# Block-sparse attention and a low-rank mixer MLP on one core: mixer sums on 32-column groups, more turns by the crossbar, a new order

## The chip, the cores and the metric

One core of a Trainium2 chip runs the whole program in one launch. The metric is the device time in microseconds (us); lower is better. A core has five engines with queues of their own: TensorE (PE in the profile, its weight loads PEld), VectorE (DVE), ScalarE (ACT), GpSimd (POOL) and SyncE (SP), which here only issues DMAs. SP and ACT can issue the DMA that turns a tile through the crossbar (DMA_TRANSPOSE).

## The reference

```python
# B, H, S, D = 4, 8, 768, 64; blocks of 32 positions
scores = q @ k.T / 8
mask   = neighbouring blocks, first and last block row and column, and 3 drawn blocks per block row
attn   = softmax(where(mask, scores, -1e9)) @ v
x = attn with the heads side by side                 # [B, 768, 512]
h = x.transpose(0, 2, 1) @ U @ V                     # U [768, 32], V [32, 768]
u = x + h.transpose(0, 2, 1)
out = u + relu(u @ w_ch1) @ w_ch2                    # 512 -> 2048 -> 512
```

Inputs and output are float32; the kernel computes in float16 with float32 sums.

## The kernel before, in words

Heads are taken in pairs: four pairs per batch, 16 in all, so pair `i` is batch `i // 4`. A sequence is held as 128 partitions by 6 chunks (`T = 6`).

The order of TensorE, VectorE, ScalarE and SP is written out by hand: the text `PLAN` is read word by word. An upper-case letter issues a TensorE step (its digit is the PSUM bank), a lower-case letter the work on another engine that takes up the oldest result of its kind. GpSimd's order is left to the framework's scheduler. The steps:

- `S` (`score`): scores of one chunk of keys of one head of batch 0, two matmuls of 384 columns; `e`: the exp on ScalarE. In batch 0 the mask is inside the contraction, as extra rows (`qres`, `kres`).
- `Q`, `H` (`two_halves`, `quad`): from batch 1 on, scores of two chunks for both heads or one; a head has 64 contraction rows, so the two heads use the two halves of the array's rows. `e` is an exp over 1536 columns, `p` a multiplication by the mask on VectorE.
- `K`, `k`: the parts of that mask.
- `A`, `V` (line 398): probabilities times values, per chunk or per head; `v` (`divide`): reciprocal and two multiplications into `xh` (float16) and `xf` (float32).
- `R` (`turn_qk`, line 644): turns q or k of a pair on TensorE, `t` copies it out. Pairs 1 to 5 are turned so; from pair 6 on `front` does it by two crossbar DMAs on SP. `Z`, `z` do the second head of pair 0.
- `M` (`mix`, line 482): `xh` times U, six matmuls per pair with U padded to 128 columns; `m` copies the result to `a16`.
- `D`, `d` (`add`): V times `a16`, three matmuls per half; two additions on VectorE, into `u16` and `xf`. After the second half `u16` is turned by the crossbar into `uT`, and from pair 4 on `loads` of the next pair is called there. `X`, `Y`, `y`, `E`, `g`: the same on TensorE for pairs 2 and 3. `T`, `x` (`turn`, line 551): pair 15's `u16` turned on TensorE.
- `U` (`w1`, line 569): four matmuls of 384 columns and a relu on ScalarE (`a`) or VectorE (`b`). The first six are in two parts: `P` with three of the four pairs, `C` with the last.
- `W` (`w2`, line 593): four matmuls of 512 columns; four `W` make one output chunk, then `f` adds `xf` and stores. The last chunk is in two halves, `L` and `l` (`last_half`, line 613). Output tiles `of` come from `opool`, which has two buffers.

`loads(i)` issues on SP the q, k and v loads of pair `i + 2` and, from pair 5 on, ahead of them the crossbar turns of pair `i + 1`; GpSimd casts what was loaded. GpSimd also issues the casting loads of W1 (behind the casts of pairs 2 and 3) and of W2 (behind those of pairs 5 and 6). `begin(i)` calls `loads(i)` when the first score of pair 0 to 4 comes up.

Of the kernel before, what the change touches and what calls it, by code (L numbers as in the profile page):

```python
# [2 lines left out]

# [18 lines left out]
def kernel(  # L22
# [43 lines left out]
    small_np = np.concatenate(  # L66
        [(ms_np - 1.0) * -MASK_BIAS, ii[:, None].astype(np.float32)], axis=1
    )

    small_dr = nc.inline_tensor(small_np, name="small_const")  # L70
    eye_dr = nc.inline_tensor(np.eye(P, dtype=np.float16), name="eye_const")
# [37 lines left out]
    small = consts.tile([P, NB + 1], FP32)  # L109
    ms = small[0:NB, 0:NB]  # L110
    iota = small[0:NB, NB:]
    id16 = consts.tile([P, P], FP16)
# [19 lines left out]
    def cast(i, dst, ld):  # L132

        if i < NPE:
            return nc.gpsimd.tensor_copy(out=dst, in_=ld)
        for h in range(2):
            for ts in (slice(0, T // 2), slice(T // 2, T)):
                last = nc.gpsimd.tensor_copy(out=dst[:, h, ts], in_=ld[:, h, ts])  # L138
        return last
# [25 lines left out]
    NPE = HP + 2  # L165
# [64 lines left out]
    with tc.manual_schedule(  # L230
# [14 lines left out]
        nc.scalar.dma_start(out=small[0:NB], in_=small_dr.ap())  # L245
        first_load(0, 1, nc.scalar)
        nc.scalar.dma_start(out=id16, in_=eye_dr.ap())
# [54 lines left out]
        first_cast(0, 0, nc.vector.tensor_copy)  # L302
        first_cast(0, 1, nc.scalar.copy)
        first_turn(1, 0)
        first_row(1, 0, nc.scalar.copy)
        mask_half(0)
        for c in range(2):
            first_turn(0, c)
            first_row(0, c, nc.scalar.copy)
        mask_row(0, 0, nc.vector.tensor_copy)  # L310
        first_turn(1, 1)
# [68 lines left out]
    slots_of = {}  # L380

    def take_est(i, h, j):

        n = free_est.pop(0)
        for u in range(2):
            slots_of[i, h, 2 * j + u] = n + u
        return n

    def drop_est(i, h, g):
        n = slots_of.pop((i, h, g))  # L390
        if g % 2:
            free_est.append(n - 1)
# [14 lines left out]
    class Batch:  # L407
        def __init__(self):
            self.xf = xpool.tile([P, T, HD], FP32, tag="xf", name="xf", bufs=2)
            self.a16 = misc.tile([P, HD], FP16, tag="a16", name="a16", bufs=2)  # L410
            self.uT = [
                upool.tile([P, S], FP16, tag=f"uT{cc}", name=f"uT{cc}")
                for cc in range(NCC)
            ]
# [6 lines left out]
    S0 S3 e Z7 e z S0 S5 e Z2 e A7 z S3 A A e S0 S5 e A R2 e S3 t R1 e A A t S5 v e S3 S1 e K6  # L421
    A0 e A k K5 S3 k A e S6 S1 e K5 A e A k A S3 v K6 R7 e k S1 t e S3 S5 e R0 e S1 t A7 A e S3
    A A e S5 K0 K2 e A k A k S3 v A0 A e S1 A S5 e A K7 e S3 k K1 R2 e k A S5 t R7 e S3 t A S1 e
    v M6 e K5 S3 m k A7 A e S1 A A e S3 D0 A e S5 d R2 e S3 t A S0 e v M6 e D2 m S3 d A5 A e S0
    K7 A e S3 k A K6 e S0 k A A e S3 v R2 e S6 t S0 e S3 e A5 A e A D7 A K6 d S1 k D0 A e S3 d
    M7 e S1 m X6 A e S3 v Y A7 e S0 y E2 A e S3 g X5 Y e E6 A y A g A A Q v R6 e e t M7 X6 m Y p
    H y R7 e p H t U6 e p H b U7 e p H b P6 p e E2 V7 g p C Q v a V6 e e U7 v p P0 a M1 C P2 m p
    a C U6 a D7 Q a d D6 e e d U7 b U6 p U0 b U7 p a E6 Q a g U7 e e U6 b P7 b p X2 C V0 a p V4
    v P5 v Y P7 y C C M0 a a W6 m D7 Q d W e e D7 W d p W U7 f p Q a U7 e e W6 b U7 p U0 b W p a
    Q W e e W p U2 f V7 a p Q v V6 e e U7 v p U0 a U2 b U6 p a M7 a Q m D7 e e W6 d W p D7 W d p  # L430
    Q W e e W7 f p U0 V6 b p V1 v U2 v U0 a U4 a M5 a U6 m D0 U1 a d D6 W a d Q U6 e e W b W p
    W6 f p Q W e e U7 W p a W p Q f U7 e e W6 b U7 p W b p Q W e e W p U0 f V7 a p Q v V6 e e U7
    v p U0 a M1 a U6 m p U4 a D3 U1 a d D7 U6 a d Q b U7 e e U6 b U7 b p U1 a V6 p a V0 v U7 v
    U4 a M3 a U7 m U6 b D4 U2 a d U7 a D6 Q a d U7 e e W6 b U7 p W a p Q U7 e e W b W p U7 f p Q
    a U7 e e W6 b U7 p U0 b U1 p b V7 a Q v W e e V7 p U0 v W a p Q M7 e e W m W7 f p D0 D6 W d
    d p W Q W e e W6 f p W V7 p V1 v U4 v U7 a M0 a U2 m D1 W a d D5 W d W7 f Q W e e W p W W6 f
    p Q U7 e e W b U7 p U2 b U0 p a W a Q U7 e e W b U7 p f U0 a U1 p a U5 a V6 a Q v V7 e e U6
    v p U1 a U0 b U7 p a M6 a Q m W7 e e D6 W d p U0 D6 U1 a d p U2 a W a Q U6 e e W b U6 p f V2
    a p U5 v V7 a U6 v U0 a M1 a U7 m D2 U0 a d D7 U6 a d Q a U6 e e W7 b W p U6 p Q a U6 e e W
    b W p U6 f p Q a U7 e e W6 b U7 p W a p Q V7 e e W v p W U7 p f Q a V7 e e W6 v p W U7 p Q a  # L440
    M7 e e W m W p D2 V7 f d p W0 v D6 W d V1 W v W M4 f W3 m D7 D0 W d d W T2 W x U7 f U6 b U0
    b U7 a U6 b U1 b U4 a U5 a U6 a U3 a U2 a W7 b U5 W a U6 U0 a U3 a W a U4 U3 b U5 b W b U4 f
    W0 a U4 U6 a U7 a U3 a U6 a U7 a U1 b W a U6 W b W W6 f W U5 U4 b U7 a U0 a U1 a W a L4 W l
    W7 f W W W W6 f W W W L7 f l
    """

    class Pair:
        def __init__(self, i, bt):
            self.i, self.bt = i, bt
            self.b, self.hp = divmod(i, HP)  # L450
            self.pu, self.pav = {}, {}
            self.xh = xpool.tile([P, T, P], FP16, tag="xh", name="xh", bufs=3)
            self.ch = slice(self.hp * P, (self.hp + 1) * P)

        def divide(self, h, pav):
            head = 2 * self.hp + h
            rcp = misc.tile([P, T], FP32, tag="rcp", name="rcp")
            nc.vector.reciprocal(out=rcp, in_=pav[:, :, D])
            for dst in (
# [3 lines left out]
                self.last = nc.vector.tensor_tensor(  # L463
                    out=dst, in0=pav[:, :, 0:D],
                    in1=rcp[:, :, None].broadcast_to([P, T, D]), op=ALU.mult,
                )

# [28 lines left out]
        def ut_a(self, c):  # L496
# [9 lines left out]
                    out=self.bt.uT[self.hp][:, c * HS : (c + 1) * HS], in_=self.pu[c]  # L506
# [3 lines left out]
        def add(self, c, n):  # L510
            if c == 0:
                self.u16 = xpool.tile([P, T, P], FP16, tag="u16", name="u16")
            pu = bank(n, [P, 3, P], FP32)
            ts = slice(3 * c, 3 * c + 3)
# [5 lines left out]
            xf = self.bt.xf[:, ts, self.ch]  # L520

            def sums():
                nc.vector.tensor_add(  # L523
                    out=self.u16[:, ts, :], in0=self.xh[:, ts, :], in1=pu
                )
                nc.vector.tensor_add(out=xf, in0=xf, in1=pu)  # L526
                if c == 1 and self.i < NPAIR - 1:
                    nc.sync.dma_start_transpose(
                        self.bt.uT[self.hp].rearrange("c (t p) -> c t p", t=T),
                        self.u16.rearrange("p t c -> p (t c)"),  # L530
                    )
                    if self.i >= HP:
                        loads(self.i + 1)
# [3 lines left out]
        def sum_only(self, c, n):  # L537
            pu = bank(n, [P, 3, P], FP32)
            ts = slice(3 * c, 3 * c + 3)
            for j in range(3):  # L540
                nc.tensor.matmul(
                    pu[:, j, :], Vt[:, 3 * c + j, :], self.bt.a16[:, self.ch],
                    start=(j == 0), stop=(j == 2), skip_group_check=True,
                )
            xf = self.bt.xf[:, ts, self.ch]
            then("g", lambda: nc.vector.tensor_add(out=xf, in0=xf, in1=pu))

        def turn(self, n):
            pt = bank(n, [P, S], FP16)
            for t in range(T):  # L550
                nc.tensor.transpose(
                    out=pt[:, t * P : (t + 1) * P], in_=self.u16[:, t, :], identity=id16
                )
            then("x", lambda: nc.vector.tensor_copy(out=self.bt.uT[self.hp], in_=pt))
# [3 lines left out]
    hold = {}  # L558

    NPART = 6  # L560
# [26 lines left out]
    def w2(b, sc, part, n=None):  # L587
        if part == 0:
            hold[b] = bank(n, [P, HD], FP32)
        po = hold[b]  # L590
# [17 lines left out]
    def last_half(c, n):  # L608
        sc = T - 1
        po = bank(n, [P, HD // 2], FP32)  # L610
        ch = slice(c * HD // 2, (c + 1) * HD // 2)
        for jj in range(NJJ):
            nc.tensor.matmul(  # L613
                po, tts[B - 1, 1, jj][:, (T // 2 - 1) * P :], w2t[:, jj, ch],
                start=(jj == 0), stop=(jj == NJJ - 1),
            )

        def finish():
            of = opool.tile([P, HD], FP32, tag="of", name="of")
            nc.vector.tensor_add(out=of[:, ch], in0=bts[B - 1].xf[:, sc, ch], in1=po)  # L620
            (nc.sync, nc.scalar)[c].dma_start(
                out=out[B - 1].rearrange("(p t) d -> p t d", t=T)[:, sc, ch],
                in_=of[:, ch],
            )
# [16 lines left out]
    def turn_qk(i, n, k_):  # L641
# [7 lines left out]

        def rows():  # L650
            if i < HP:
                augs[i] = (qres[i % 2], kres[i % 2])
                for h in range(2):
                    nc.vector.tensor_copy(  # L654
                        out=augs[i][n][drows[h], h, :], in_=pt[drows[h], :]
                    )
            else:
                nc.vector.tensor_copy(out=plain(i)[n], in_=pt)
# [180 lines left out]
```

## Time and profile before

| | |
|---|---|
| time, median of 10 runs | 286.2 us (285.33 to 286.81) |
| the profiled execution: time, span | 286.31 us, 284.4 us |
| TensorE clock granted | 1.0 throughout |
| busy: PE, DVE, ACT, POOL | 277.3, 197.4, 179.2, 70.2 us |
| data moved by DMA | 36.78 MB, mean 129 GB/s |

The span runs from the first to the last instruction; 1.9 us of the time lie around it. A row of the timeline reads: start, length, engine, line, operation, tile written from tiles read, shapes, count, and in brackets the idle time before it and what ended it. A matmul's length holds its way through the array, so in a row of n matmuls all but the last overlap the next one's. A row of a stretch lists the engines' busy time in it, with the number of instructions in brackets, then the granted clock, the mean share of the DMA engines, and GB/s.

### The profile page before, as it was taken

How to read it: one execution, taken by the hardware profiler on the slowest of the kernel's cores; microseconds unless marked ns; L12 is line 12 of the kernel's file. 1: busy time of each engine (PE TensorE's matmuls, PEld its weight loads, DVE VectorE, ACT ScalarE, POOL GpSimd, SP SyncE). 2: the span in 40 equal slices, each digit the busy share in tenths (PEclk: the TensorE clock that was granted, in tenths of full speed). 3: DMA queues.
4: the chain of work that ended last, by engine and by line, in shares of the span. 5: the costliest groups of instructions: out<-in, count | busy, mean ns of one | idle time of the engine just before them, and what ended most of it. 6: DMA issues, size and time to landing. Idle time of an engine off the chain costs nothing.

```text
span 284.4 us, 6730 instructions
## 1 busy us (share of the span) xinstructions
PE 277.3 (98%) x2770; PEld 163.6 (58%) x2770; DVE 197.4 (69%) x360; ACT 179.2 (63%) x213; POOL 70.2 (25%) x160
## 2 busy tenths in 40 slices
PE   8799999999999999999999999999999999999995
PEld 3567775657456654567555564565745565555553
DVE  5588989998768966788686975666866888231121
ACT  4899998885768466675776527777588730424200
POOL 5485233902251043401361032600310000000000
PEclk9999999999999999999999999999999999999999
DMA  5799999599370578108460498303741103001012
GB/s 182 224 310 277 218 208 230 113 148 234 76 246 6 102 239 242 70 14 227 96 203 2 104 234 205 141 7 65 221 86 39 39 37 90 13 0 40 37 55 92
DMA packets 46466, 36.78 MB, mean 129 GB/s; under 512 B 28036, under 2 KB 42948, under 8 KB 46436
## 3 DMA queue, kind: packets, MB, share of 16 engines
q1 hardware_dynamic: 43280, 31.80, 41.7%
q0 software_dynamic: 2688, 4.19, 8.3%
q8 instruction: 21, 0.34, 0.5%
q10 hardware_dynamic: 468, 0.36, 0.4%
q14 instruction: 9, 0.07, 0.1%
HBM read 27.66 MB, written 6.29 MB: 119 GB/s over the span
## 4 chain that ended last, share of the span: by engine, by line
PE 86%; DVE 6%; DMA 4%; POOL 1%; SPq 1%; issue 1%; DVEq 0%; POOLq 0%
PE ps L569 29%; PE ps L593 28%; PE ps L398 11%; PE ps L692 9%; DMA kld<-in_k_dram 4%; PE ps L669 3%; PE ps L482 2%; PE ps L516 2%; PE ps L613 1%; DVE xh L463 1%; DVE mask L636 1%; DVE xf L463 1%; DVE est L707 1%; DVE u L523 1%; PE ps L644 1%
## 5 line engine op out<-in xcount | busy, mean ns | idle before, releaser
L701 ACT ACTIVATE est<-ps 128x1536 f16<-128x1536 f32 x72 | 100.4, 1449 | 31.3 <-PE ps L692 31.3
L569 PE MATMUL ps<-uT,w1t 128*128 128x384 f16 x512 | 95.6, 326 | 0.4 <-DVE xf L526 0.2
L593 PE MATMUL ps<-w2t,tT 128*128 128x512 f16 x368 | 88.8, 379 | 0.0
L707 DVE TENSOR_TENSOR est<-est,mask 128x1536 f16<-128x1536 f16 x72 | 69.5, 968 | 13.3 <-ACT est L701 13.0
L581 ACT ACTIVATE tT<-ps 128x384 f16<-128x384 f32 x87 | 42.2, 493 | 54.0 <-PE ps L569 52.5
L569 PEld LDWEIGHTS <-w1t 128*128 128x128 f16 x512 | 47.4, 98 | 36.8 <-issue 6.6
L593 PEld LDWEIGHTS <-tT 128*128 128x128 f16 x368 | 34.4, 98 | 36.5 <-issue 2.9
L398 PEld LDWEIGHTS <-est 128*128 128x128 f16 x1152 | 40.7, 97 | 7.0 <-issue 1.2
L138 POOL CAST stqld<-qld 128x192 f16<-128x192 f32 x40 | 16.7, 458 | 111.7 <-DMA qld<-in_q_dram 111.7
L583 DVE TENSOR_SCALAR tT<-ps 128x384 f16<-128x384 f32 x41 | 22.8, 555 | 30.6 <-PE ps L569 30.0
L398 PE MATMUL ps<-vt,est 128*128 128x65 f16 x1152 | 43.3, 193 | 0.2
L678 ACT ACTIVATE est<-ps 128x768 f16<-128x768 f32 x48 | 34.9, 813 | 2.0 <-PE ps L669 2.0
L692 PE MATMUL ps<-qpl,kpl 64*128 64x512 f16 (+1 forms) x288 | 31.3, 325 | 0.0
L669 PE MATMUL ps<-qres,kres 128*128 128x384 f16 x96 | 22.2, 324 | 0.8 <-DVE kres L654 0.4
L601 DVE TENSOR_TENSOR of<-xf,ps 128x512 f32<-128x512 f32 x23 | 15.7, 685 | 9.8 <-PE ps L593 9.6
L692 PEld LDWEIGHTS <-kpl 64*128 64x128 f16 x288 | 11.7, 94 | 15.4 <-issue 9.5
L523 DVE TENSOR_TENSOR u<-xh,ps 128x384 f16<-128x384 f16 x28 | 15.4, 551 | 6.8 <-PE ps L516 6.1
L463 DVE TENSOR_TENSOR xh<-ps,rcp 128x384 f16<-128x384 f32 x32 | 17.8, 558 | 1.1
L463 DVE TENSOR_TENSOR xf<-ps,rcp 128x384 f32<-128x384 f32 x32 | 17.5, 548 | 0.0
L138 POOL CAST vt<-vld 128x192 f16<-128x192 f32 x40 | 15.2, 421 | 3.5 <-PE ps L692 2.3
L138 POOL CAST stkld<-kld 128x192 f16<-128x192 f32 x40 | 15.6, 430 | 0.4 <-DMA kld<-in_k_dram 0.4
L526 DVE TENSOR_TENSOR xf<-xf,ps 128x384 f32<-128x384 f32 x28 | 15.3, 548 | 0.0
(81 smaller groups left out, 142.8 us busy)
## 6 DMA issues: line engine op xcount, KB each, us to landing
vld<-in_v_dram SPq DMA_DIRECT2D x16, 384.0 KB, 4.6
out_dram<-of SPq DMA_DIRECT2D x23, 256.0 KB, 2.0
qld<-in_q_dram SPq DMA_DIRECT2D x15, 384.0 KB, 5.9
kld<-in_k_dram SPq DMA_DIRECT2D x15, 384.0 KB, 7.0
w1t<-in_moe_w_ch_dram POOLq DMA_DIRECT2D x4, 512.0 KB, 10.5
w2t<-in_moe_w_ch_dram POOLq DMA_DIRECT2D x4, 512.0 KB, 7.4
qld<-in_q_dram SPq DMA_DIRECT2D x2, 192.0 KB, 2.3
uT<-u SPq DMA_TRANSPOSE x13, 2.8
```

The lines of the kernel that those rows point to most:

```text
L138: last = nc.gpsimd.tensor_copy(out=dst[:, h, ts], in_=ld[:, h, ts])
L398: nc.tensor.matmul(pav[:, sc, :], est[:, n, sc * P : (sc + 1) * P], vts[b % 2][:, 2 * hp + h, g, 0 : D + 1], start=(g == 0 and sc == 0), s ...
L463: self.last = nc.vector.tensor_tensor(out=dst, in0=pav[:, :, 0:D], in1=rcp[:, :, None].broadcast_to([P, T, D]), op=ALU.mult,)
L569: nc.tensor.matmul(pt, w1t[:, cc, jj * P : (jj + 1) * P], bts[b].uT[cc][:, c * HS : (c + 1) * HS], start=(cc == 0), stop=(cc == NCC - 1), ...
L581: nc.scalar.activation(out=dst, in_=pt, func=AF.Relu)
L583: nc.vector.tensor_scalar_max(out=dst, in0=pt, scalar1=0.0)
L593: nc.tensor.matmul(po, tts[b, c, jj][:, s * P : (s + 1) * P], w2t[:, jj, :], start=(jj == 0), stop=(jj == NJJ - 1),)
L669: nc.tensor.matmul(ps[:, c], kT[:, h, g * P : (g + 1) * P], qT[:, h, c * HS : (c + 1) * HS], start=True, stop=True,)
L678: lambda: nc.scalar.activation(out=dst, in_=ps, func=AF.Exp, scale=0.125),
L692: nc.tensor.matmul(units[h][:, u * S + lo : u * S + hi], kT[drows[h], g * P : (g + 1) * P], qT[drows[h], lo:hi], start=True, stop=True, sk ...
L701: nc.scalar.activation(out=both[h], in_=units[h].rearrange("p (g n) -> p g n", g=2), func=AF.Exp, scale=0.125,)
L707: lambda: nc.vector.tensor_mul(out=both[h], in0=both[h], in1=mask[:, 2 * j : 2 * j + 2, :]),
```

## The change

- The identity matrix comes in the same DMA as the other constants (128 rows of 356 bytes), on ACT's queue ahead of k. At the start q and k are both cast on VectorE, and q is turned before k.
- `B` (`two_scores`) takes two chunks of batch 0 in three banks with one exp of 1536 columns. The order has nine `B` and 30 `S` where it had 48 `S`.
- `M` for batches 1 to 3 is `mix_all`: once per batch, 24 matmuls with 32 weight columns each, spread over four groups of 32 output partitions; the four partial sums are added by the next contraction, for which V is copied to the other three row groups of `Vt` (three DMAs on SP, when pair 6 begins).
- The `D` of a batch therefore stand together at its end. They sum into `xh` (six buffers) in place of `u16`, and all of them turn it by the crossbar; `T` is gone.
- Pair 5 is turned by the crossbar, issued when pair 4 begins. `loads` of the next pair is called after the division of a pair's second head.
- `loads(2)` comes with `loads(1)`. All of W1 is loaded behind pair 3's k cast; all of W2 behind four small GpSimd copies that wait for pair 5's turned k (`hold`).
- `P` takes two pairs, `C` the other two.
- The second half of the last chunk is two quarters with an addition and a store each.
- `PLAN` is new; the relus are 90 `a` and 38 `b` for 87 and 41.

```diff
+    small_np = np.zeros((P, NB + 1 + P // 2), np.float32)
+    small_np[:, NB + 1 :] = np.eye(P, dtype=np.float16).view(np.float32)
...
-        nc.scalar.dma_start(out=small[0:NB], in_=small_dr.ap())
+        nc.scalar.dma_start(out=small, in_=small_dr.ap())
         first_load(0, 1, nc.scalar)
-        nc.scalar.dma_start(out=id16, in_=eye_dr.ap())
...
-        first_cast(0, 0, nc.vector.tensor_copy)
-        first_cast(0, 1, nc.scalar.copy)
-        first_turn(1, 0)
-        first_row(1, 0, nc.scalar.copy)
-        mask_half(0)
+        for n in range(2):
+            first_cast(0, n, nc.vector.tensor_copy)
         for c in range(2):
             first_turn(0, c)
             first_row(0, c, nc.scalar.copy)
+        mask_half(0)
         mask_row(0, 0, nc.vector.tensor_copy)
+        first_turn(1, 0)
+        first_row(1, 0, nc.scalar.copy)
...
         def divide(self, h, pav):
...
+            if h and self.i >= HP:
+                loads(self.i + 1)
...
+        def add(self, c, n):
+            pu = self.part_of_mix(c, n)
...
             def sums():
-                nc.vector.tensor_add(
-                    out=self.u16[:, ts, :], in0=self.xh[:, ts, :], in1=pu
-                )
+                nc.vector.tensor_add(out=xh, in0=xh, in1=pu)
                 nc.vector.tensor_add(out=xf, in0=xf, in1=pu)
-                if c == 1 and self.i < NPAIR - 1:
+                if c == 1:
                     nc.sync.dma_start_transpose(
...
+    def mix_all(b, n):
+        bt = bts[b]
+        pa = bank(n, [P, HD], FP32)
+        tiles = [[(c, hp) for hp in range(HP)] for c in range(4)]
+        for c in range(4):
+            tiles[c] += [(4 + c // 2, 2 * (c % 2) + u) for u in range(2)]
+        for m in range(HP + 2):
+            for c in range(4):
+                sc, hp = tiles[c][m]
                 nc.tensor.matmul(
+                    pa[c * R : (c + 1) * R, hp * P : (hp + 1) * P],
+                    Ut[:, sc, 0:R], bt.xh[hp][:, sc, :],
+                    start=(m == 0), stop=(m >= HP), skip_group_check=True,
+                )
+        then("m", lambda: nc.vector.tensor_copy(out=bt.a16, in_=pa))
...
     def last_half(c, n):
         sc = T - 1
+        parts_ = [(slice(0, HD // 2), nc.sync)] if c == 0 else [
+            (slice(HD // 2, HD * 3 // 4), nc.scalar),
+            (slice(HD * 3 // 4, HD), nc.sync),
+        ]
+        po = bank(n, [P, HD], FP32)
...
         def finish():
+            for ch, queue in parts_:
+                of = opool.tile([P, HD], FP32, tag="of", name="of")
+                nc.vector.tensor_add(
+                    out=of[:, ch], in0=bts[B - 1].xf[:, sc, ch], in1=po[:, ch]
+                )
+                queue.dma_start(
+                    out=out[B - 1].rearrange("(p t) d -> p t d", t=T)[:, sc, ch],
+                    in_=of[:, ch],
+                )
...
+    SPANS = ((0, 0, 512), (0, 512, S), (1, 0, 256), (1, 256, S))
+
+    def two_scores(i, h, g, n):
+        ps = PS[:, n : n + 3, :].rearrange("p b n -> p (b n)")
+        qT, kT = augs[i]
+        s = take_est(i, h, g, g + 1)
+        for u, lo, hi in SPANS:
+            nc.tensor.matmul(
+                ps[:, u * S + lo : u * S + hi],
+                kT[:, h, (g + u) * P : (g + u + 1) * P],
+                qT[:, h, lo:hi],
+                start=True, stop=True, skip_group_check=True,
+            )
+        then(
+            "e",
+            lambda: nc.scalar.activation(
+                out=est[:, s : s + 2, :], in_=ps.rearrange("p (g n) -> p g n", g=2),
+                func=AF.Exp, scale=0.125,
+            ),
+        )
...
     def loads(i):
         behind = ExitStack()
-        if NPE <= i + 1 < NPAIR:
+        if HP + 1 < i + 1 < NPAIR:
             behind.enter_context(tc.issue_after(front(i + 1).ins))
         if i + 2 < NPAIR:
             with behind:
                 last = load_qk(i + 2)
                 load_v(i + 2)
...
+            if i == 1:
+                with tc.issue_after(last.ins):
+                    load_w1(range(NCC))
+
+    def hold(behind):
+        for j in range(0, NJJ, 4):
+            nc.gpsimd.tensor_copy(out=w2t[0:1, j, 0:1], in_=behind[0:1, 0:1])
+        load_w2(range(0, NJJ, 4))
...
     def begin(i):
...
-        if i <= HP:
-            loads(i)
+        if i == HP:
+            front(HP + 1)
+        elif i == HP + 2:
+            for c in range(1, 4):
+                nc.sync.dma_start(out=Vt[c * R : (c + 1) * R], in_=Vt[0:R])
+        for m in {0: (0,), 1: (1, 2), 3: (3,), 4: (4,)}.get(i, ()):
+            loads(m)
+        if i == HP:
+            hold(kpl[1])
...
-        "R": ((turn_qk, i, n) for i, n in each(range(1, NPE), (0, 1))),
+        "R": ((turn_qk, i, n) for i, n in each(range(1, HP + 1), (0, 1))),
```

The new `PLAN` up to the sixth `Q`, and its end:

```
S0 S3 e e S5 B0 e Z7 e S3 z Z6 e z B0 A7 A e R6 S3 t A R5 e A B0 t A K6 e A S3 k v A5 A e K6
k B0 A A e K7 A K6 k S3 k A K7 e v B0 k S3 e M6 e A5 A m R7 A t B0 K6 R3 e k A A t S6 A e v
S0 D2 S3 e d A7 A e A S0 K6 A e S3 k K2 A e S5 k A e v S3 R2 e S5 t S0 e M7 e S3 m D2 e B5 d
A0 D1 e A A d A S3 D2 A e d K1 S5 k R7 e S3 t A S1 e v A5 A e A S3 S6 e K2 A e A k A S3 v B0
e K7 M6 e k S3 m X5 K7 e A6 Y k A B0 y X7 Y e S3 y E5 A e A g A R7 S0 t A e v S4 S2 e A7 A e
R1 E6 A t A g A A Q v e e M6 X7 m Y P6 y p H U7 e p H b C e p H b U7 e p H b U6 e p E1 a g p
V7 Q v e e V6 U7 v p U0 a P1 b C p P6 a C E7 Q a g U6 e e U7 b P6 b p U0 C a U7 p a Q b X6 Y
e e P7 y C P6 b C p U0 b a p V7 Q v e e V6 W7 v p U0 W a p Q U6 e e W b U6 p W b p Q f W6 e
...
b W a U0 U7 b U1 b W a L4 f W2 l W W W W4 f W W W L7 f l
```

## The prediction

> **What bounds the kernel now.** I read the page first: busy shares, slices, chain of waits.
>
> ```profile
> span 284.4 us, 6730 instructions
> ...
> PE 277.3 (98%) x2770; PEld 163.6 (58%) x2770; DVE 197.4 (69%) x360; ACT 179.2 (63%) x213; POOL 70.2 (25%) x160
> ...
> PE   8799999999999999999999999999999999999995
> ...
> DVE  5588989998768966788686975666866888231121
> ACT  4899998885768466675776527777588730424200
> ...
> PE 86%; DVE 6%; DMA 4%; POOL 1%; SPq 1%; issue 1%; DVEq 0%; POOLq 0%
> ```
>
> TensorE is in the chain for 86%, but its neighbours are also full in the first third. So I asked for the busy time by stages, cut at the first score of batch 0 (6.6), the pair-1 load wait (14.3), the first Q step (43.8), the third (63), the sixth (75.4), the last pair's crossbar-free turn (238.3) and the end of matmuls.
>
> ```profile
> 14.30:43.80 29.50, 28.86 (x424) 21.27 (x423) 26.18 (x60) 28.99 (x40) 14.50 (x20) 1.00 0.99 247
> 43.80:63.00 19.20, 18.63 (x200) 10.93 (x200) 18.60 (x34) 16.64 (x17) 9.03 (x16) 1.00 1.02 176
> ...
> 75.40:238.30 162.90, 162.85 (x1657) 93.20 (x1657) 122.55 (x210) 106.79 (x114) 36.39 (x96) 1.00 0.45 120
> 238.30:281.20 42.90, 42.90 (x251) 24.11 (x249) 11.48 (x20) 10.31 (x21) 0.00 (x0) 1.00 0.10 35
> ```
>
> (Columns: stretch, length, busy of PE, PEld, DVE, ACT, POOL.) To 43.8 ScalarE has 28.99 of 29.50 us: exps bound it. To 63 VectorE has 18.60 of 19.20. After 75.4 only TensorE counts, and work taken from it there is time saved. Then the timeline, for step costs, the start and the tail.
>
> ```profile
> 4.17 0.51 ACT L209 CAST stkld<-kld 128x384 f16<-128x384 f32 x1 [0.29 <-DMA kld<-in_k_dram]
> 4.78 0.36 PE L223 MATMUL ps<-id,stkld 128*64 128x128 f16 x3 [0.43 <-DMA id<-eye_const]
> 7.15 5.08 ACT L678 ACTIVATE est<-ps 128x768 f16<-128x768 f32 x7 [0.57 <-PE ps L669]
> 12.02 0.51 PE L644 MATMUL ps<-id,stqld 128*128 128x128 f16 x6 [0.85 <-POOL stqld L135]
> 12.89 0.81 ACT L678 ACTIVATE est<-ps 128x768 f16<-128x768 f32 x1 [0.66 <-PE ps L669]
> 14.29 8.02 ACT L678 ACTIVATE est<-ps 128x768 f16<-128x768 f32 x11 [0.59 <-PE ps L669]
> ```
>
> ```profile
> 154.11 0.82 PE L692 MATMUL ps<-qpl,kpl 64*128 64x512 f16 x8
> 154.86 0.51 PE L482 MATMUL ps<-xh,Ut 128*128 128x128 f16 x6
> 155.21 1.24 PE L593 MATMUL ps<-w2t,tT 128*128 128x512 f16 x5
> ```
>
> ```profile
> 279.33 1.91 PE L613 MATMUL ps<-w2t,tT 128*128 128x256 f16 x16
> 279.53 0.69 DVE L601 TENSOR_TENSOR of<-xf,ps 128x512 f32<-128x512 f32 x1 [2.71 <-PE ps L593]
> 281.28 0.42 DVE L620 TENSOR_TENSOR of<-xf,ps 128x256 f32<-128x256 f32 x1 [1.06 <-PE ps L613]
> 281.73 0.34 ACTq L621 DMA_DIRECT2D out_dram<-of  x1
> ```
>
> A step costs its start-to-start time, not its busy time, which ends in 0.2 us of pipeline. Six 128-column matmuls: (0.51-0.219)/5, about 56 ns each, 0.34 us a step (M, R, T). A Q lasts 154.86-154.11 = 0.75; its eight matmuls use two row groups at once (0.66), the rest, 0.09, is the switch back to the whole array; entering costs as much (M at 88.71 to Q at 89.14 is 0.43, not 0.34). From the chain: U 0.65, W 0.86, V 1.09 (36 load-and-matmul pairs, 30.4 ns each), A a sixth of V, S 0.33.
>
> **The change, part by part.** I counted both order texts with these costs. Up to the first Q both hold the same: 48 score chunks, 48 A, 12 K, 8 R, 2 Z, 3 M, 4 D and the X, Y, E: 32.4 us of TensorE. From there to the last matmul: 235.0 us before, where the trace takes 281.1-43.8 = 237.3, so 2.3 us of waits; after, 232.7. The difference is three edits.
>
> 1. Pair 5 turned by the crossbar: two R go, -0.67; its two 0.56 us copies leave VectorE.
> 2. Pair 15 likewise: T goes, -0.34.
> 3. Mixer sums: twelve M (4.03) become three of 24 matmuls on 32 weight columns. No row shows a 32-column weight. Ends: four groups truly at once, 6 x 56 ns = 0.34; one after another, 24 x 56 = 1.34; two switches add 0.19. The nearest row is V's: a load and a short matmul every 30.4 ns, so 0.73 + 0.19 = 0.92 a sum and 2.76 for three: -1.27 (ends -2.4 and +0.6). The Trainium skill speaks against: TensorEngine Tiling (Array Packing), Restrictions, says that column tiling gives up the fast weight load, and Key Properties that a change of mode drains the array. The second is the measured 0.09. For the first, TensorE: Matmul & The Clock Gate, LDWEIGHTS, gives columns/1.2 ns: 27 ns for 32, 0.64 for 24, so under my 0.73. The same page's table of measured packing (three column tiles 2.38 times faster) would make 24 x 56/2.38 = 0.56, +0.19 = 0.75, another -0.5 in all. I stay with the trace's row. On VectorE twelve copies of 0.29 become three of about 0.69.
>
> 4. Start. 45.6 KB of constants instead of 2.3 KB go ahead of k on ACT's queue: 43 KB at the 300 GB/s of the slices, k some 0.15 us later. But the identity comes with them (the first turn waited 0.43 for it), k is cast on VectorE (0.36, as q's row) instead of ScalarE (0.51), and q's turn and rows no longer queue behind k's. First exp about 6.65 for 7.15 (bounds 6.4 and 7.3).
>
> 5. Exps. A single takes 0.72 in the x11 row (8.02 less the 0.1 overlap, by 11); a double, like L701 pairs (2.79 for two, mean 1.45), about 1.35. Each B saves 0.1, nine 0.9. Pair 1's q still comes at 12.02 and holds R6 and what follows, but by then eight chunks are done instead of seven; walking the new order (S S S B S, B, wait, S, wait, B, S) gives 12 chunks by 16.3, where before has them at 17.3. The remaining 36: 24 x 0.72 + 6 x 1.36 = 25.4; before they take 26.2. That is 41.7, and 0.3 for the last A: first Q at 42.0. TensorE, with 32.4 of work and some 2.3 of load waits, could not be there before 41.3; two full engines wait for one another, so I add 0.5: 42.5 for 43.8, -1.3 (bounds 0 and -2).
>
> 6. From the first Q to the sixth: before, VectorE has 14 p, 5 v, 4 d, 6 b, 2 t, 3 m and the y, g, f: 32.7 us (p 0.97, v 1.3, d 1.1, b 0.56) against 29.9 of TensorE; it takes 31.6. After, D moves behind the batch and 9 b come: 27.6 against 26.1. VectorE still lags, by half as much: waits 0.9 for 1.7, -0.8. The d come back in clumps of eight late in each batch; between the 23rd and 26th Q VectorE has 16.7 us beside 18.8, so it is covered.
>
> 7. Tail. The last half is cut into two quarters, 32 x 56 ns = 1.79 for 1.75. Each quarter takes an `of` buffer, and there are two. The last quarter's buffer is that of the last whole output (L601's 279.53 add), whose store must have landed: add ends at 0.9 after the last L begins, landing 2.0 to 2.4 later by the store row. So the last add starts at 3.1 instead of 1.95; it is shorter (0.29 for 0.42) and moves 64 KB. Net +0.8 (bounds -0.15, if no such wait, and +1.1).
>
> At nothing: W1 all behind pair 3's k cast (four issues of 0.6 on POOL; from about 23 us, landing in up to 12.8, so 38; first needed by P at 44; late by x costs x). Pair 5's two crossbar issues hold SP 1.2 us each ahead of pair 6's loads: rows by 47, needed at 51.3. Pair 6: loads issued at 46, landed 53, cast 57, turned by 60, needed at 64.3. Loads now issue at `v` instead of behind D, so later pairs have 4 us or more. Three Vt copies hold SP 0.8 each at pair 6, covered until the batch's D at 96. Batch ends: the last D lies 8 to 10 us ahead of the first U that reads it; sums 2.2 and crossbar 2.8 leave 3 us or more. `xh` summed in place, three more relu on ScalarE: both idle enough.
>
> Sum: -0.67 -0.34 -1.27 -1.3 -0.8 +0.8 = -3.6 on the profiled execution's 286.31 (span 284.4 and 1.9 around it; the median of ten is 286.2): **282.7**.
>
> **Rivals.**
> *W2 too late (slower).* `hold` makes POOL wait for pair 5's crossbar rows, and pair 6's casts share that queue. If the holds queue behind pair 6's last cast (58.5), W2's four issues of 0.74 start at 59. Before, the four W1 transfers, under similar traffic, took from 19.1 to 36.8: 17.7. So the last quarter lands at 76.9, where the fourth W needs it at 71.5: 5.4 us of standing TensorE, 288.1. It decides from 75 on, and begins to cost at 71.5. For: POOL's 111.7 us of waits for q loads. Against: the holds are ready at 47, the casts only at 53.
> *Column groups dear.* In line: 284.6; with a switch of 0.09 at each of the 72 matmuls, +8: 290.7. Against: Q alternates row groups eight times without it.
> *The first stage does not shrink.* Doubles need three banks at once, the new order may starve ScalarE: first Q at 43.8 and VectorE's waits as before: 284.8.
>
> **How the numbers follow.** Forecast 0.66, all of it faster; first stage 0.13 (0.09 faster, 0.02 same, 0.02 slower); groups 0.08 (0.02, 0.01, 0.05); W2 0.13 (0.02, 0.03, 0.08). About 0.2%, 0.57 us, can be told from no change. Faster 0.79, same 0.06, slower 0.15. The forecast with its bounds (mix -1.1, tail -0.9, first Q -0.7, not all together) begins at 280.6; W2 late by some 4 us ends at 286.9.
>
> **What would show it.** First Q near 42.5; mix groups of 0.9 us, no R for pair 5, no T; the L601 add before the last one followed by a VectorE wait of over 1 us for a store; no TensorE wait for w2t between 66 and 77. A first Q past 43.8, or a TensorE gap at W, would prove me wrong.

## The result, and the profile after

The changed kernel takes 284.17 us (median of 14 runs, 283.47 to 288.11), the kernel before 286.21 us; the ratio is 0.9932, with a 95% interval of 0.9916 to 0.9947. It is faster by 0.7%, 2.0 us; 282.7 us was forecast. Its runs do not agree as closely as those of before. With those of e1_same below there are 34: 16 lie at 283.1 to 283.8 (called the usual ones here), eight at 284.7 to 285.1, eight at 285.8 to 287.0, two above. Where there are profiles, this goes with when TensorE gets its full clock, which is the second half of this story.

The profiled execution, 286.32 us with a span of 284.4, is one of the long ones. From its page, of the whole span:

```profile
span 284.4 us, 6704 instructions
...
PE 276.9 (97%) x2768; PEld 161.6 (57%) x2768; DVE 194.0 (68%) x347; ACT 178.2 (63%) x206; POOL 74.3 (26%) x164
...
PE 92%; DVE 3%; DMA 2%; ACT 1%; issue 0%; SPq 0%; DVEq 0%; ACTq 0%
```

TensorE's part of the chain of waits rises from 86 to 92%: less else is left in it. The second profile of the same kernel (run e1_same, 283.23 us, span 281.3) shows a usual run. Cut at its own first Q, sixth Q and last L (columns: stretch, length, busy of PE, PEld, DVE, ACT, POOL):

```profile
14.30:43.26 28.96, 28.54 (x426) 21.38 (x424) 26.38 (x59) 27.54 (x32) 14.18 (x19) 1.00 1.02 254
43.26:70.42 27.16, 26.95 (x299) 15.54 (x297) 24.59 (x44) 22.57 (x22) 14.97 (x33) 1.00 1.12 205
70.42:274.92 204.50, 204.50 (x1917) 114.49 (x1917) 133.83 (x222) 118.47 (x140) 39.04 (x96) 1.00 0.37 104
```

and the kernel before at the same three steps:

```profile
14.30:43.80 29.50, 28.86 (x424) 21.27 (x423) 26.18 (x60) 28.99 (x40) 14.50 (x20) 1.00 0.99 247
43.80:75.40 31.60, 31.03 (x344) 18.47 (x344) 28.58 (x53) 23.86 (x24) 12.57 (x28) 1.00 0.87 164
75.40:279.30 203.90, 203.85 (x1891) 115.84 (x1891) 133.34 (x228) 117.10 (x135) 36.39 (x96) 1.00 0.38 103
```

Between these two executions, both at the full clock from 4.9 us on, the first Q comes 0.53 us earlier, the middle stretch is 4.44 shorter, the long one 0.60 longer (work has moved from the one to the other), and the tail, below, 1.37 longer: 3.0 us in all. VectorE is as full in the middle stretch as it was, 24.59 of 27.16 us for 28.58 of 31.60. The medians differ by 1.0 us less than these two executions; as far as profiles show, that is lost in the start. The waits of TensorE's matmuls in e1_same (us in total, times, longest) are all there too, ahead of 11 us:

```profile
PE ps L264 <- PEq L885: 0.8, 1, 0.8
PE ps L716 <- DVE kres L344: 0.7, 1, 0.7
PE ps L224 <- DVE stqld L210: 0.6, 1, 0.6
PE ps L697 <- DVE kres L279: 0.5, 1, 0.5
```

### The profile page after: what moved, and what is told of

It is laid out like the page before. It is cut to its first block, busy times and chain, and to the rows that moved or that the text cites. A ratio compares the mean times of both kernels' runs of the same rounds, so it can differ in the third digit from the quotient of the medians.

```text
span 284.4 us, 6704 instructions
## 1 busy us (share of the span) xinstructions
PE 276.9 (97%) x2768; PEld 161.6 (57%) x2768; DVE 194.0 (68%) x347; ACT 178.2 (63%) x206; POOL 74.3 (26%) x164
## 4 chain that ended last, share of the span: by engine, by line
PE 92%; DVE 3%; DMA 2%; ACT 1%; issue 0%; SPq 0%; DVEq 0%; ACTq 0%
PE ps L587 30%; PE ps L611 28%; PE ps L400 12%; PE ps L741 10%; PE ps L697 3%; PE ps L716 2%; PE ps L529 2%; DMA qld<-in_q_dram 1%; PE ps L656 1%; DMA out_dram<-of 1%; DVE qres L686 1%; PE ps L636 1%; PE ps L670 1%; PE ps L224 1%; ACT est L724 1%
## 5 line engine op out<-in xcount | busy, mean ns | idle before, releaser
L587 PE MATMUL ps<-uT,w1t 128*128 128x384 f16 x512 | 94.3, 326 | 0.0
L611 PE MATMUL ps<-w2t,tT 128*128 128x512 f16 x368 | 87.1, 379 | 0.0
L599 ACT ACTIVATE tT<-ps 128x384 f16<-128x384 f32 x90 | 43.0, 494 | 43.5 <-PE ps L587 42.3
L601 DVE TENSOR_SCALAR tT<-ps 128x384 f16<-128x384 f32 x38 | 21.1, 556 | 19.0 <-PE ps L587 18.3
L706 ACT ACTIVATE est<-ps 128x768 f16<-128x768 f32 x30 | 22.4, 811 | 1.5 <-PE ps L697 1.5
L741 PEld LDWEIGHTS <-kpl 64*128 64x128 f16 x288 | 11.8, 94 | 15.9 <-issue 10.4
L140 POOL CAST stkld<-kld 128x192 f16<-128x192 f32 x40 | 18.1, 491 | 0.7 <-PE ps L400 0.7
L541 DVE TENSOR_TENSOR xh<-xh,ps 128x384 f16<-128x384 f16 x28 | 15.4, 550 | 1.7 <-PE ps L529 1.6
L697 PE MATMUL ps<-qres,kres 128*128 128x384 f16 x60 | 15.1, 351 | 0.3
```

Of the source, the lines that this page charges most:

```text
L587: nc.tensor.matmul(pt, w1t[:, cc, jj * P : (jj + 1) * P], bts[b].uT[cc][:, c * HS : (c + 1) * HS], start=(cc == 0), stop=(cc == NCC - 1), ...
L599: nc.scalar.activation(out=dst, in_=pt, func=AF.Relu)
L601: nc.vector.tensor_scalar_max(out=dst, in0=pt, scalar1=0.0)
L611: nc.tensor.matmul(po, tts[b, c, jj][:, s * P : (s + 1) * P], w2t[:, jj, :], start=(jj == 0), stop=(jj == NJJ - 1),)
L697: nc.tensor.matmul(ps[:, c], kT[:, h, g * P : (g + 1) * P], qT[:, h, c * HS : (c + 1) * HS], start=True, stop=True,)
L706: lambda: nc.scalar.activation(out=dst, in_=ps, func=AF.Exp, scale=0.125),
```

## The experiments

Every kernel below but e9_before is the changed kernel with the edit named; times are medians, and their ratios are against the kernel before, run beside them.

**The changed kernel again (e1_same).** No edit.

> The changed kernel unedited, for a second profile and the spread of its times. Clock theory: the start has two or more outcomes, set by when TensorE gets its full clock (12.9 us in the profile at hand against 4.9 before); a run with the full clock before 8 us has its first Q near 43 and takes about 283.5 us, one with 12.9 takes 286.3. Load theory: first Q always near 46, the time set by when q lands (4.8 us), spread under 0.5 us.

Measured: 284.79 us over 20 runs (283.08 to 289.49), 0.9933 (0.9909 to 0.9957). The two profiles of one program differ at the start. First the long execution:

```profile
4.82 0.36 DVE L210 CAST stqld<-qld 128x384 f16<-128x384 f32 x1 [1.30 <-DMA qld<-in_q_dram]
5.24 0.85 PE L224 MATMUL ps<-small,stqld 128*64 128x128 f16 x6 [0.88 <-DVE stqld L210]
8.05 2.13 PE L697 MATMUL ps<-qres,kres 128*128 128x384 f16 x6
...
13.94 0.82 PE L716 MATMUL ps<-qres,kres 128*128 128x512 f16 x4 [0.72 <-DVE kres L344]
```

then the usual one:

```profile
4.55 0.36 DVE L210 CAST stqld<-qld 128x384 f16<-128x384 f32 x1 [1.03 <-DMA qld<-in_q_dram]
4.97 0.52 PE L224 MATMUL ps<-small,stqld 128*64 128x128 f16 x6 [0.61 <-DVE stqld L210]
6.64 0.99 PE L697 MATMUL ps<-qres,kres 128*128 128x384 f16 x5
...
10.84 0.82 PE L716 MATMUL ps<-qres,kres 128*128 128x512 f16 x4 [0.72 <-DVE kres L344]
```

Six turns take 0.85 us in the one and 0.52 in the other. Six score matmuls take 2.13 where five take 0.99, which is 0.33 and 0.165 us from one start to the next: in the long execution the array still runs at half its clock. The trace's record of the granted clock begins with the full clock, at 12.9 us in the one and at 4.9 in the other. (The rows of stretches count the time ahead of that record as full clock, so their 1.00, and the "1.0 throughout" of the kernel before, say nothing of these first microseconds.) The first Q follows at 46.35 and 43.26, and from there on the two are the same to 0.1 us: 27.16 to the sixth Q, then 204.5 to the last L, then 6.40 to the end. So all of the spread of this pair is made in the first 13 us. The clock theory stands; load theory's "always near 46" falls.

**The constants split again (e2_split).**

```diff
-        nc.scalar.dma_start(out=small, in_=small_dr.ap())
+        nc.scalar.dma_start(out=small[0:NB, 0 : NB + 1], in_=small_dr.ap()[0:NB, 0 : NB + 1])
         first_load(0, 1, nc.scalar)
+        nc.scalar.dma_start(out=small[:, NB + 1 :], in_=small_dr.ap()[:, NB + 1 :])
```

> Undoes one part: the 24 rows of small constants go ahead of k, the identity behind it, as before; all else as changed. Both theories: q lands near 3.6 us again and is cast by 4.0. Clock theory: no idle time of TensorE long enough to lose the clock, full clock by 5 us, first Q near 42.5 to 43, all runs near 283 or less. Load theory: 1.2 us less than the changed kernel whatever the clock does.

Measured: 283.13 us (283.01 to 285.87, 7 runs), 0.9913 (0.9882 to 0.9944). q is cast at 3.52 instead of 4.55, so both theories have that right; but the first turn then waits for the identity until 4.69, and the first Q comes at 43.22, where the usual run of the changed kernel has 43.26. One transfer for the constants is worth nothing at the start: what it gains on the identity it loses on q. Load theory's 1.2 us are not there: its usual runs, 283.01 to 283.25, lie at the low end of the changed kernel's, 283.08 to 283.83. One run of seven is still at 285.87, so the split does not shut out the late clock either.

**More warming (e3_warm10).** `keep_warm(8)` becomes `keep_warm(10)`.

> Ten warming matmuls for eight, so TensorE runs on to 5.2 us, when q's cast is done; the constants still in one transfer. Clock theory: q late as before, but full clock by 8 us in every run, first Q near 43, median 283.5 and no run at 286. Load theory: no difference from the changed kernel (within 0.2 us).

Measured: 283.62 us (283.39 to 286.3, 9 runs), 0.9921 (0.9896 to 0.9947). Full clock at 4.3 us, first Q at 43.56. The median is as the clock theory said; that no run would be at 286 was wrong, by one.

**No warming (e10_cold).** `keep_warm(8)` is taken out.

> The changed kernel without its eight warming matmuls ahead of q; the two of 256 columns stay. Clock theory: full clock only from 8 to 13 us in every run, first Q from 44.4 to 46.4 (as in the three profiles whose clock came at 9.9, 12.2 and 12.9), time 284.5 to 287, hardly a run at 283.4. Load theory: no difference.

Measured: 285.76 us, all ten runs between 285.13 and 286.38; 0.9984 (0.9968 to 1.0001), no longer faster than before. Its profile has the full clock at 10.4 us and the first Q at 45.17. The loads are untouched (q is cast at 4.88 us), and the usual times are gone, so the clock alone can lengthen a run by this much.

**TensorE at work throughout the start (e11_hot).**

```diff
-        keep_warm(8)
+        keep_warm(10)
...
         mask_half(0)
+        keep_warm(2, 256)
...
-        keep_warm(2, 256)
+        keep_warm(4, 256)
```

> The changed kernel with TensorE kept at work through the start: ten warming matmuls for eight, two short ones after the first mask half, four for two ahead of the first score. Clock theory: full clock by 6.5 us in every run, so the times close up: 283.2 to 284, none at 286. If the late clock has nothing to do with idle time of TensorE: the same spread, and some 0.2 us more for the extra matmuls.

Measured: 284.06 us, five runs of six between 283.84 and 284.29, one at 285.61; 0.993 (0.9908 to 0.9952). The times close up, for 0.5 us more in the usual run: full clock at 4.8 but first Q at 43.96. With one of six still late, filling the gaps makes the late clock rarer at best; six runs can't say by how much.

**k on SP behind q (e5_k_sp).** `first_load(0, 1, nc.scalar)` becomes `first_load(0, 1, nc.sync)`.

> k's first half is issued on SP behind q's instead of on ACT; the constants stay in one transfer. Queue theory: q is late in the changed kernel because k's load is now issued ahead of it (1.13 against 1.26 us) and takes turns with it; then q lands near 3.6, its first turn starts near 4.0 (the identity is there), first exp near 6.6 for 7.2, and the time is 0.3 to 0.6 us less than the changed kernel's usual 283.4, with fewer runs at 286. Size theory: the 45 KB of constants themselves delay q; then q still lands past 4.3 and nothing is gained.

Measured: 283.41 us (282.59 to 284.48, 6 runs), 0.9904 (0.9882 to 0.9925). The start of its profile:

```profile
3.77 0.36 DVE L210 CAST stqld<-qld 128x384 f16<-128x384 f32 x1 [0.25 <-DMA qld<-in_q_dram]
4.29 0.85 PE L224 MATMUL ps<-small,stqld 128*64 128x128 f16 x6
7.11 2.13 PE L697 MATMUL ps<-qres,kres 128*128 128x384 f16 x6
```

q lands 0.8 us earlier with the 45 KB of constants loaded as in the changed kernel: about q's arrival the queue theory is right and the size theory wrong. k's load, issued 0.13 us ahead of q's on the other queue, holds q up, though k itself then lands after q (at 4.7 us in e1_same, where q is cast at 4.55).

The time is less clear. TensorE has no idle time here from 0.8 to 11.3 us, and yet the full clock came only at 9.9; the turns took 0.85, the first score came at 7.11 (6.64 in e1_same) and the first Q at 44.41. So this profile shows no gain. But the shortest run, 282.59, is 0.5 us below all 34 of the changed kernel, and no run is at 286: with an early clock an early q may be worth the forecast 0.3 to 0.6 us. No profile of such a run was taken.

**Sums on the whole array (e6_mix_full).**

```diff
-                    pa[c * R : (c + 1) * R, hp * P : (hp + 1) * P],
-                    Ut[:, sc, 0:R], bt.xh[hp][:, sc, :],
+                    pa[:, hp * P : (hp + 1) * P],
+                    Ut[:, sc, :], bt.xh[hp][:, sc, :],
...
```

(the loops around it now go pair by pair)

> Undoes one part: the batch's mixer sums by 24 matmuls on the padded 128 columns, one after another, all else as changed. By the trace (24 grouped matmuls in 0.35 us, four at a time, 0.45 with a switch): each sum 24 x 56 ns = 1.34, so 0.9 to 1.0 more for each of three, 2.7 to 3.0 us slower than the changed kernel. By the prediction's row (0.92 grouped): 1.3 slower. If the sums are covered: no difference.

Measured: 287.46 us (285.59 to 288.73, 12 runs), 1.0043 (1.0019 to 1.0068): slower than the kernel before. One batch's sum in e1_same, between a Q and a W:

```profile
94.99 0.52 PE L566 MATMUL ps<-xh,Ut 128*32 128x128 f16 x24
95.44 1.25 PE L611 MATMUL ps<-w2t,tT 128*128 128x512 f16 x5
```

and in e6_mix_full:

```profile
95.00 1.51 PE L562 MATMUL ps<-xh,Ut 128*128 128x128 f16 x24
96.35 1.03 PE L608 MATMUL ps<-w2t,tT 128*128 128x512 f16 x4
```

From the start of the sum to the start of the W it is 1.35 us against 0.45; the 0.45 holds the switch back to the whole array, and the 1.35 has none. From the sixth Q to the last L it is 207.14 for 204.50, 2.64 for three sums, and the first Q is the same to 0.01. The shortest runs, 285.59 to 286.34, lie 2.5 above the usual ones of the changed kernel. At the medians the column groups alone carry more than the whole gain; of the 3.0 us between the two early-clock executions above they carry 2.64.

**Two exps for one (e7_two_exps).**

```diff
...
-                out=est[:, s : s + 2, :], in_=ps.rearrange("p (g n) -> p g n", g=2),
...
+                out=est[:, s + u, :], in_=ps[:, u * S : (u + 1) * S],
...
```

(for `u` in 0 and 1)

> Undoes one part: the two chunks of a B step keep their three banks but take an exp each, so nine pairs of 768 columns for nine of 1536. Prediction's step 5: 0.9 us slower, the first stage being bound by ScalarE. Rival, from the changed kernel's trace, where ScalarE stood idle for 1.1 us ahead of doubles and TensorE was busy 26.45 of 26.80 us: the first exp of a pair needs only the first two matmuls, the waits shrink, and the difference is under 0.4 us.

Measured: 284.14 us (283.12 to 287.65, 7 runs), 0.9923 (0.9895 to 0.995); its three shortest runs, 283.12 to 283.26, are those of the changed kernel (283.08 to 283.31). Its profile is of a long run (full clock at 12.2 us), so the times decide. The double exps bring nothing that can be told: the rival is right. In e1_same ScalarE stood idle ahead of four doubles:

```profile
ACT est L724 <- PE ps L716: 1.1, 4, 0.4
```

(the waits of ScalarE from 16 to 43.5 us: total, times, longest). A double is 0.1 us cheaper than two singles and starts only when both chunks are scored: nine should gain 0.9, and 1.1 is lost in waits ahead of them.

**Three output buffers (e4_of3).** `opool` has `bufs=3`.

> Three output buffers for two: takes away the wait of the last quarter's addition for the store of the chunk before. By the prediction's step 7: 0.8 to 0.9 us less than the changed kernel, the last addition starting 2.0 us after the last L begins instead of 3.1. If the tail's end is set by the last store of a whole chunk anyway: under 0.2 us.

Measured: 283.27 us (282.57 to 285.56, 12 runs), 0.9913 (0.9887 to 0.9939). The tail of e1_same:

```profile
274.92 1.95 PE L636 MATMUL ps<-w2t,tT 128*128 128x128 f16 x32
275.12 0.69 DVE L619 TENSOR_TENSOR of<-xf,ps 128x512 f32<-128x512 f32 x1 [2.71 <-PE ps L611]
276.91 0.29 DVE L644 TENSOR_TENSOR of<-xf,ps 128x128 f32<-128x128 f32 x1 [1.10 <-PE ps L636]
277.95 0.29 DVE L644 TENSOR_TENSOR of<-xf,ps 128x128 f32<-128x128 f32 x1 [0.75 <-DMA out_dram<-of]
278.26 0.33 SPq L647 DMA_DIRECT2D out_dram<-of  x1
```

and of e4_of3:

```profile
275.14 1.95 PE L636 MATMUL ps<-w2t,tT 128*128 128x128 f16 x32
...
277.13 0.49 DVE L644 TENSOR_TENSOR of<-xf,ps 128x128 f32<-128x128 f32 x2 [1.10 <-PE ps L636]
277.45 0.34 ACTq L647 DMA_DIRECT2D out_dram<-of  x1
277.64 0.33 SPq L647 DMA_DIRECT2D out_dram<-of  x1
```

The wait for a store in brackets is gone; the last L to the end is 5.63 instead of 6.40, and the usual runs move from about 283.4 to 282.65.

**The mends together (e8_k_sp_of3).** k on SP, three buffers.

> k on SP behind q, and three output buffers: the two mends together. If both work and add up: 0.3 to 0.6 and 0.8, so about 282.2 us in most runs and no slower mode at the start; if k on SP does nothing, the time of the kernel with three buffers alone (most runs 282.65).

Measured: 282.89 us (282.21 to 285.09, 6 runs), 0.99 (0.9869 to 0.9932), the best median of all, and below that of both kernels. Against e4_of3 alone six runs do not settle a difference. In its profile q is cast at 3.58, but the full clock comes at 6.3 us and the first Q at 43.30, no earlier than in e1_same. Its shortest run, 282.21, is 0.4 us below that of e4_of3 (282.57), as e5_k_sp's was below the changed kernel's; no profile shows why.

**The last store's queue (e12_act_last).** As e8_k_sp_of3, with the third quarter on SP and the last on ACT.

> k on SP behind q, three output buffers, and the last two quarter stores change queues: the third quarter on SP, the last on ACT. From the last issue to the end takes 3.1 us where SP issues 64 KB, and 2.6 us before, where ACT issued 128 KB. If the queue makes the difference: 2.6, so 0.4 to 0.5 us less than the same with SP last (most runs 282.2 to 282.9). If the shorter rows do: no difference.

Measured: 284.0 us (282.05 to 284.6, 6 runs), 0.9913 (0.9883 to 0.9942); its profile has the late clock (9.9). The tail alone answers the question: the last issue at 278.57, the end of the span at 281.6, so 3.0 us, where SP last takes 3.1. The queue is not it. The shorter rows (512 bytes for 1 KB) are left over, but were not tried by themselves, and neither was a last store without another one just ahead of it.

**The kernel before again (e9_before).**

> The kernel before, unedited, for a second profile: the full clock begins near 5 us or earlier, first Q near 43.5, the last L 235.5 us after it, the end 5.0 us after that; time 285.5 to 286.5.

Measured: 286.84 us (285.83 to 287.1, 8 runs), 1.0016 (0.9998 to 1.0034). The expectation that its clock always comes early is wrong: full clock at 9.7 us. But its first Q comes at 44.10, only 0.31 later than with the clock at 4.9. With the new order a clock at 9.9 costs 1.15 (44.41 in e5_k_sp and e12_act_last, which have k on SP besides, for 43.26 in e1_same). What the two timelines of before show fits the difference; the early clock first:

```profile
12.02 0.51 PE L644 MATMUL ps<-id,stqld 128*128 128x128 f16 x6 [0.85 <-POOL stqld L135]
```

```profile
12.34 0.50 PE L644 MATMUL ps<-id,stqld 128*128 128x128 f16 x6
```

Before, TensorE stands 0.85 us for pair 1's load at 12 us; a slow start uses up that wait, and most of the loss is hidden (1.15 less 0.85 is 0.30). In e1_same the same turn starts at 11.86 without a wait, and a slow start is paid in full. That is read from the timelines; no run puts the wait back.

## Why the prediction was right or wrong, point by point

The direction, the range and the mechanism (TensorE's work taken out of the stages that TensorE bounds) were right. The size was 1.5 us off at the median. That it is no further off is in part luck: the mixer sums brought 1.4 us more than forecast, the first stage, the waits and the tail together 1.9 less, and the late clocks take another 1.0 from the median. By the prediction's own sign, a first Q past 43.8, the profiled execution (46.35) would prove it wrong; e1_same (43.26) would not. The term that makes the difference, the clock at the start, is not in the prediction at all.

- **Steps 1 and 2**, the two crossbar turns (-0.67, -0.34): the turns are gone from the trace (`L670` has 48 matmuls where `L644` had 60, and there is no `turn`), and no TensorE wait for the crossbar took their place. Neither was undone by itself; their size is argued from the 56 ns a matmul (the prediction's own working gives 58; e6_mix_full measures 1.35 us for 24, so 56).
- **Step 3**, the mixer sums, is the term most mis-sized: -1.27 forecast, -2.64 by e6_mix_full, whose 24 matmuls in line cost what the twelve M did (3 x 1.35 for 4.03). The step that failed is the choice of V's row as the nearest: 30.4 ns per load and matmul was taken for a floor. The four groups go truly at once: in the trace of e1_same four matmuls start within 11 ns, and the next four 56 ns after them, so 24 take 0.52 us with the 0.2 of pipeline. That end of the range was within the trace's reach, since Q already showed two row groups at once. It was even too dear by one switch: the sum follows a Q, whose 0.75 holds the switch already. The estimate from the Trainium skill, TensorE: Matmul & The Clock Gate, Part 3, 0.75 us a sum from its measured packing, was nearer to the measured 0.45, and too high as well; and the loss of the fast weight load that TensorEngine Tiling (Array Packing), Restrictions, names shows no cost here.
- **Step 4**, the start: the first exp was put at 6.65; it comes at 7.18 in the usual run, as before. The step took q's arrival as unchanged and let only k slip. q slips too, by 0.9 us, because k's load is now issued first (e5_k_sp). And the clock was not thought of: the warming matmuls end at 4.36, and the first turn comes at 4.97 to 5.24.
- **Step 5**: twelve chunks by 16.3 was right (16.2 in e1_same), but the 36 after that take 26.8 us, not 25.4 and 0.5 for the two engines' waits on one another. ScalarE's own work is as forecast (25.64 us); the doubles' 0.9 is taken back by the 1.1 of waits ahead of them (e7_two_exps), for TensorE, 28.54 of 28.96 us busy, is fuller than ScalarE. The first Q comes at 43.26 in the usual run, for 42.5, and at 44.4 to 46.4 with a late clock. This is the miss on the losing side, and the one that varies.
- **Step 6**: first to sixth Q forecast at 27.0, measured 27.16.
- **Step 7**, the tail: the buffer's wait is there, 0.75 in its row and 0.77 by e4_of3, where +0.8 was forecast for the whole. The wait that was to be over 1 us was shorter, but the tail is 1.37 longer, because the step took the smaller last store for no slower: 64 KB need 3.1 us from issue to the end where 128 KB needed 2.6. Even with three buffers the tail is 5.63, for 5.03 before the change.
- **Sum**, in the usual run against the profiled execution of before: -1.0 -2.64 -0.53 (first Q) +1.37 is -2.8, which leaves -0.2 of the 3.0 for the waits and whatever else the new order changes, where -0.8 was forecast. The last L starts at 274.92, and the forecast's terms put it at 274.9: there 1.4 more from the sums meets 0.8 less from the first Q and 0.6 less from the waits, which is the luck.
- **Rivals**: W2 was not late enough: its last quarter lands at 70.3 in e1_same, the fourth W starts at 73.35, and TensorE has no wait for it. Column groups were the opposite of dear. That the first stage would not shrink (0.13) is what happened in most of it, at 0.5 instead of 1.3.

**What stays open.** Why one execution gets the full clock at 4.9 and the next of the same program at 12.9. In the fourteen profiles it begins at 3.6 to 6.3 us (eight of them) or at 9.7 to 12.9 (six), never between. The Trainium skill, TensorE: Matmul & The Clock Gate, Part 1, says that the clock is granted by how busy TensorE was in a window of 3.4 us that runs free of the program. The traces agree with the window: in all fourteen the stretch of full clock lasts a whole number of steps of 3.413 us (79 to 82), so it begins and ends on a grid. Where the grid lies differs from execution to execution, and the late clock goes with it: of the eleven profiles with eight warming matmuls, the five with a grid point at 0.15 to 1.87 us have the early clock, and of the six with one at 1.96 to 3.11 only e8_k_sp_of3 does (at 6.3). So a window that takes in too little of the warming seems to be missed, by chance. No run sets the grid, and how much work a window must hold is not shown: e5_k_sp, with TensorE never idle ahead of it, missed one too. e10_cold shows only that work ahead of q decides how often it is missed.

## What to carry to other kernels

A narrow stationary operand (32 columns) in four column groups is worth its switch even for a few dozen matmuls: three sums of 24 fell from 4.0 to 1.35 us. Here the four partial sums cost TensorE nothing more, since the next contraction adds them up in matmuls as long as before (219 ns each). When a wait is removed at the start of a kernel, look at what it hid: here it seems to have hidden a cold array, and the shorter order pays for each late clock. Cutting the last store in two did not pay: the smaller piece did not land sooner, and the tail is longer than before the change even with a buffer for each piece (5.63 us for 5.03). The uncut last half in the new order was not run.

## What the runs showed of the hardware that was not expected

- 24 matmuls of 128 columns, each with its own 32-column load, start four at a time in four column groups, a group every 56 ns (13 ns a matmul); on the whole array they start 56 ns apart one by one.
- The full clock of TensorE begins at 4.9 us in one execution of the changed kernel and at 12.9 in another, at 4.9 and 9.7 in two of the kernel before; in the changed kernel that is worth 3.1 us of the first Q. The time at full clock is a whole number of steps of 3.413 us in every profile.
- Two first loads on two queues delay one another: k issued 0.13 us ahead of q has q cast at 4.5 to 4.9 us. q is cast at 3.5 to 3.7 where k follows it by 0.11 to 0.12 us on the other queue (before, e2_split), and at 3.6 to 3.8 where k follows it on the same queue.
- A last store of 64 KB in rows of 512 bytes takes 3.0 to 3.1 us from issue to the end of the span, one of 128 KB in rows of 1 KB 2.6.
